# Moving the batch sums, the second step's loads and its normalization in the paired attention steps of a fused attention and gated-MLP kernel

## The chip, the cores and the metric

The kernel runs on one core of a Trainium2 chip. The metric is the device time of one execution in microseconds (us), lower is better. The kernel before takes 518.73 us (median of three runs). Engines are named as the profile names them: PE (TensorE's matmuls), PEld (its weight loads), DVE (VectorE), ACT (ScalarE), POOL (GpSimd), SP (SyncE, which here only issues DMAs).

## The reference

Attention over 4 batches, 8 heads, 768 positions and 64 dimensions, where each query sees the keys within 15 positions and 24 block summaries (the maximum of 32 keys, the mean of 32 values), and behind it a gated network on the 3072 tokens:

```python
k_sum = k.reshape(B, H, nb, block, D).max(axis=3)       # block = 32
v_sum = v.reshape(B, H, nb, block, D).mean(axis=3)
scores_l = scale * np.matmul(q, k.transpose(0, 1, 3, 2))  # masked to |i - j| < 16
scores_s = scale * np.einsum('bhsd,bhnd->bhsn', q, k_sum) + np.log(block)
a = softmax(concatenate([scores_l_masked, scores_s]))
x = a @ concatenate([v, v_sum])                          # 3072 tokens x 512
out = ((x @ w1) * (x @ w2)) @ w3 @ w_out                 # 512 -> 1024 -> 1024 -> 512
```

## The kernel before, in words

Tokens are worked in six units of 512, and a unit has four attention steps, one for each pair of heads: 24 steps in all. A step s stands for `divmod(s, 4)`, unit and pair. One step makes the scores of 512 queries against 120 columns each (96 keys and 24 summaries) on PE (L375), takes the row minima and the mask on DVE (`reduce`, L389), the exponentials and their sums on ACT (`expose`, L403), the reciprocals (`invert`, L408 on ACT and L409 on DVE), multiplies by them (the normalization), transposes the weights on PE (L433), copies the transposes out (`evacuate`, one half on ACT at L438 and one on DVE at L442), and multiplies by the values on PE (`outputs`, L453).

The first eight steps are worked one by one early on. The other sixteen come in pairs: the paired step m, from 4 to 11, holds the steps a = 2m and b = 2m + 1 (`two_steps`). For each m, in program order: `turned(m - 1)` transposes the two steps before and evacuates them, `run` gives PE 18 x 512 columns of the network's matmuls (LEAD), `two_steps` finishes the two steps before with their output products, makes the scores of a and b, and then places the vector work in blocks, with `run(given[0] + LEAD / 2)` (nine matmuls) between them, and at last runs the network until `begins(m + 1) - LEAD`.

The network's matmuls are one long stream (`stream`, taken in order by `run`), on 512 columns each. Up to `CLASSIC` columns it is the folding of the two last weights (w3 and w_out, into `wp`) and the network for the first two units (`gate`, `project`, all at L125); behind it come the other four units in two groups of seven products each (`lanes`, at L736), which read their weights from DRAM tile by tile (`ws`, L781 and L866, six buffers). `begins` sets at which column of the stream a paired step starts: up to m = 8 in equal parts between `TO_SLOTS + LEAD` and `CLASSIC + BEFORE_FAST`, and after that every `BETWEEN` columns. `FAST` is 12,288 columns, or 24 matmuls.

Batches 2 and 3 need their own summaries. Their sixteen loads (four of keys, four of values for each batch, 392 and 512 KB each) and the reductions over them are the later batches' work. `load_batch` issues two loads (L261, L276), `reduce_batch` reduces the two that are under way (L266 for keys, L283 and L284 for values). The loads have two buffers (`raw`), so a load waits until the reduction of the one two before it has read its buffer. Each paired step does both twice: once behind `invert` of step b and once at the middle of the network's stretch. The sixteen are done by m = 7.

How the queues get their order: PE's and POOL's are the program's order. Between `with tc.manual_schedule(engines=vector)` blocks the compiler's scheduler orders ACT, DVE and SP by readiness in its own model and by priority, which is the place in the program; `tc.high_priority(offset=SOONER)` moves an instruction ahead by 400 places. Inside such a block ACT and DVE keep the written order; the instructions of other blocks can stand between them. All loads go through SP's one queue, which issues in order: an issue that waits for its buffer holds up all behind it. Beside the sixteen loads these are a step's values (`fetch_values`, three DMAs at L325, two buffers), queries and keys (`fetch`, L340 and L342, two buffers each), the value summaries (`fetch_means`, L358), and the network's weights. `fill` (L362, POOL) writes the key summaries into a step's keys once these have landed.

The network's background work (`sums_of_gates`, `sums_of_output`, `moving`) makes sums and differences of 512-column tiles on DVE (L121, L634, L685, L691, L938) and casts on ACT, and DVE also adds up what `lanes` leaves in PSUM (L756, L813).

Of the kernel before, what the change touches and what calls it, by code (L numbers as in the profile page):

```python
# [16 lines left out]
ALU = mybir.AluOpType  # L17
# [3 lines left out]
P = 128  # L21
# [31 lines left out]
SOONER = 400  # L53
# [20 lines left out]
def attention_moe(ctx, tc, qG, kW, kT, vP, vW, vB, mask, w1, w2, w3T, wo, out, outT):  # L74
    nc = tc.nc
    B, NPAIR, _, S = kT.shape
# [5 lines left out]
    NI = 2 * NBLK  # L82
# [3 lines left out]
    KR = CUT + NB  # L86
# [40 lines left out]
    def aligned(shape, **more):  # L127


        n = math.prod(shape[1:])  # L130
        step = 32 if more["bufs"] % 4 == 0 else 64
        t = sb.tile([shape[0], -(-n // step) * step], F32, **more)[:, :n]
        return t.rearrange("p (a b) -> p a b", b=shape[2]) if len(shape) == 3 else t
# [185 lines left out]
    def load_values(u, p):  # L319


        v = sb.tile([P, 2, NBLK, P], F32, name="v", bufs=2)

        for g, rows in ((0, slice(0, CUT)), (1, slice(0, CUT - 64)), (1, slice(CUT + NB - 64, KR))):
            nc.sync.dma_start(v[rows, g], vW[u, p, rows, g])  # L325
        return v
# [9 lines left out]
    def load_scores(u, p):  # L336

        q = sb.tile([P, U], F32, name="q")
        k = sb.tile([P, NBLK, COLS], F32, name="k")
        nc.sync.dma_start(q, qG[p, :, u * U : (u + 1) * U])  # L340
        if u:
            nc.sync.dma_start(k, kW[p, :, u * NBLK : (u + 1) * NBLK])  # L342
        return q, k
# [82 lines left out]
    def transposes(sm, **more):  # L426

        tp = [ps.tile([P, 512], F32, name="tp", **more or {"bufs": 2}) for _ in range(2)]
        for j in range(NI):
            for g in range(2):  # L430
                rows = slice(64 * g, 64 * g + 64)
                to, p = tp[g][:KR, j * 64 : j * 64 + 64], sm[rows, j]
                nc.tensor.transpose(to, p, ident[rows, rows])  # L433
        return tp

    def evacuate(tp, second="V"):
        pt = [sb.tile([KR, U], F32, name="pt", bufs=6) for _ in range(2)]
        nc.scalar.copy(pt[0], tp[0][:KR, :U])  # L438
        if second == "A":
            nc.scalar.copy(pt[1], tp[1][:KR, :U])  # L440
        else:
            nc.vector.tensor_copy(pt[1], tp[1][:KR, :U])  # L442
        return pt
# [531 lines left out]
    given, tended = [0.0], [0.0]  # L975

    def tend():


        some = False  # L980
        for works in (tasks, background):
            while works:
                n = next(works[0], 0)
                if n > 0:
                    return True
                if n < 0:
                    break
                works.pop(0)
                some = True
        return some  # L990

    def run(columns):

        while given[0] < columns:
            n = next(stream, 0)
            if n <= 0:
                if n == 0 or not tend():
                    return
                continue
            given[0] += n  # L1000
            if given[0] >= tended[0]:
                tended[0] = max(tended[0] + 4.5 * U, given[0])
                tend()

    def place(s):
        return divmod(s, NPAIR)
# [3 lines left out]
    def fetch(s):  # L1010
        if s < NS:
            inputs[s] = load_scores(*place(s))

    def fetch_values(s):
        if s < NS:
            values[s] = load_values(*place(s))
# [9 lines left out]
    def begin(s):  # L1026
        u, p = place(s)
        sm = sb.tile([P, NI, KR], F32, name="sm", tag="wf", bufs=5)
        mx = aligned([P, 3, NI], name="mx", bufs=4)
        sms[s] = sm, mx  # L1030
        return u, sm, mx, scores(*inputs.pop(s))
# [13 lines left out]
    def load_batch():  # L1045
        for _ in range(2 if later_batches else 0):
            load_, work = later_batches.pop(0)
            under_way.append((work, load_()))

    def reduce_batch():  # L1050
        for work, raw in under_way:
            work(raw)
        under_way.clear()
# [183 lines left out]
    FAST = 3 * U * 4 * KH  # L1237
    LEAD = 18 * U
    PAIRS = range(NFIRST // 2, NS // 2)
    BEFORE_FAST = 0.8 * FAST  # L1240
    BETWEEN = 3.0 * FAST

    def begins(m):

        if m <= NFIRST:
            return TO_SLOTS + LEAD + (CLASSIC + BEFORE_FAST - TO_SLOTS - LEAD) * (m - PAIRS[0]) / (NFIRST - PAIRS[0])
        return CLASSIC + BEFORE_FAST + BETWEEN * (m - NFIRST)

# [9 lines left out]
    def turned(m):  # L1258

        with tc.manual_schedule(engines={engines.Activation, engines.DVE}):  # L1260
            tps = [transposes(sms.pop(p)[0], **SPARE) for p in (2 * m, 2 * m + 1)]
            return [evacuate(tp) for tp in tps]

    def normalize_both(steps):
        for _, sm, mx, _ in steps:
            nc.gpsimd.tensor_tensor(sm, sm, mx[:, 2].unsqueeze(2).broadcast_to([P, NI, KR]), ALU.mult)  # L1266

    def two_steps(m, pts):

        two = (2 * m, 2 * m + 1)  # L1270
        vector = {engines.Activation, engines.DVE}
        with tc.manual_schedule(engines=vector):
            for p, pt in zip(two, pts):
                finish_step(p - 2, pt, **SPARE)
            if m not in PAIRS:
                return
            steps = [begin(p) for p in two]
            (u, sm, mx, sc), (u2, sm2, mx2, sc2) = steps
            reduce(u, 0, sc, sm, mx)
            expose(0, sm, mx)  # L1280
            reduce(u, 1, sc, sm, mx)
        for p in two:
            fetch_values(p)
        for p in two:
            fetch(p + 2)
        for work in EXTRA.get((m, 0), ()):
            work()
        run(given[0] + LEAD / 2)
        with tc.manual_schedule(engines=vector):
            expose(1, sm, mx)  # L1290
            reduce(u2, 0, sc2, sm2, mx2)
            invert(mx)
        run(given[0] + LEAD / 2)
        with tc.manual_schedule(engines=vector):
            expose(0, sm2, mx2)
            reduce(u2, 1, sc2, sm2, mx2)
        normalize_both(steps[:1])
        run(given[0] + LEAD / 2)
        with tc.manual_schedule(engines=vector):
            expose(1, sm2, mx2)  # L1300
            invert(mx2)
            reduce_batch()
        normalize_both(steps[1:])
        load_batch()
        until = begins(m + 1) - LEAD
        run((given[0] + until) / 2)
        for p in two:
            fill(p + 2)
            fetch_means(*place(p), values[p])
        with tc.manual_schedule(engines=vector):  # L1310
            reduce_batch()
        load_batch()
        for work in EXTRA.get((m, 1), ()):
            work()
        run(until)
# [78 lines left out]
```

## Time and profile before

| what | us |
|---|---|
| median of three runs | 518.73 |
| lowest, highest | 518.18, 520.55 |
| the profiled execution, its own time | 516.49 |
| span from its first to its last instruction | 514.7 |
| PE busy | 485.8 (94% of the span) |
| PEld busy | 395.3 (77%) |
| DVE busy | 376.7 (73%) |
| ACT busy | 275.1 (53%) |
| POOL busy | 74.5 (14%) |

The span is counted from the first to the last instruction; 1.79 us of the profiled execution lie around it. A busy PE is not PE at its peak, so its stalls are read from the idle time in front of its instructions and from the granted clock of a stretch, 1.00 being 2.4 GHz and 0.50 being 1.2 GHz. The paired steps lie between about 150 and 350 us of the span.

### The profile page before, as it was taken

To read this page: it belongs to the slowest core of one execution; us is meant where nothing else is said; L and a number is where in the kernel's file an instruction comes from. 1 tells how busy PE (TensorE), PEld (TensorE's weight loads), DVE (VectorE), ACT (ScalarE), POOL (GpSimd) and SP (SyncE) were. 2 spreads that over 40 slices of the span, in tenths; PEclk is the share of its full clock that TensorE was granted. 3 is DMA by queue.
4 is the path that set the end of the run, shared out by engine and by line. 5 is a ranking of instruction groups with operands and counts; after the bars stand their busy time and mean duration, and the time that the engine had idled before them with its cause. 6 is when DMAs were issued, how large, how long until landed. Compare 5 with 4: busy or idle time off the path is not lost. (4 is left out here: it accounts for less than half of the span.)

```text
span 514.7 us, 10411 instructions
## 1 busy us (share of the span) xinstructions
PE 485.8 (94%) x3804; PEld 395.3 (77%) x3804; DVE 376.7 (73%) x889; ACT 275.1 (53%) x738; POOL 74.5 (14%) x101
## 2 busy tenths in 40 slices
PE   0989999999999997899899998999999999999997
PEld 0667777888878886788687886888787888888886
DVE  4969886897616867856988898699999019229972
ACT  5589864875726472727484558451835421522720
POOL 1034523000212313111212304020000000000000
PEclk9999999999999999899899999999999999999999
DMA  8998697999699988869887979998768766556752
GB/s 344 412 408 263 224 356 263 371 401 363 188 300 262 274 260 234 244 205 306 324 276 259 323 263 306 374 293 280 246 217 279 238 200 197 181 193 206 200 190 102
DMA packets 57603, 139.28 MB, mean 271 GB/s; under 512 B 6224, under 2 KB 19280, under 8 KB 54992
## 3 DMA queue, kind: packets, MB, share of 16 engines
q1 hardware_dynamic: 55248, 134.43, 76.9%
q0 software_dynamic: 1152, 2.10, 2.9%
q10 hardware_dynamic: 1152, 2.10, 1.1%
q8 instruction: 30, 0.49, 0.4%
q14 instruction: 21, 0.17, 0.1%
HBM read 105.89 MB, written 32.70 MB: 269 GB/s over the span
## 5 line engine op out<-in xcount | busy, mean ns | idle before, releaser
L736 PE MATMUL ln<-xT,ws 128*128 128x512 f32 x672 | 158.3, 395 | 2.3 <-DMA ws<-wS 2.0
L736 PEld LDWEIGHTS ln<-xT,ws 128*128 128x128 f32 x672 | 126.5, 190 | 30.3 <-ACT hr L754 2.4
L125 PE MATMUL mm<-x,w 128*128 128x512 f32 x384 | 89.3, 392 | 0.2 <-DVE g L527 0.2
L125 PEld LDWEIGHTS mm<-x,w 128*128 128x128 f32 x384 | 71.4, 188 | 16.2 <-DVE g L527 0.6
L403 ACT ACTIVATE sm<-sm,mx 128x120 f32<-128x120 f32 x192 | 73.5, 387 | 9.7 <-DVE mx L389 7.7
L736 PE MATMUL ln<-hT,ws 128*128 128x512 f32 (+1 forms) x348 | 77.2, 383 | 0.1
L736 PEld LDWEIGHTS ln<-hT,ws 128*128 128x128 f32 x348 | 63.7, 188 | 13.5 <-ACT tmp L754 0.5
L756 DVE TENSOR_TENSOR tmp<-ln,tmp 128x512 f32<-128x512 f32 (+1 forms) x53 | 35.7, 675 | 50.5 <-ACT tmp L754 35.1
L125 PE MATMUL mm<-w,w 128*128 128x512 f32 x192 | 50.3, 412 | 14.6 <-ACT w L220 12.0
L638 ACT CAST hT<-hr 128x512 fp32r<-128x512 f32 x56 | 32.1, 621 | 53.4 <-DVE hr L813 42.0
L125 PEld LDWEIGHTS mm<-w,w 128*128 128x128 f32 x192 | 36.2, 195 | 25.7 <-ACT w L220 12.8
L1266 POOL TENSOR_TENSOR sm<-sm,mx 128x960 f32<-128x960 f32 x16 | 29.2, 1827 | 142.0 <-DVE mx L409 133.6
L125 PE MATMUL mm<-wp,h 128*128 128x512 f32 x192 | 45.4, 393 | 0.0
L389 DVE CUSTOM_DVE_ANT_0 sm<-sc,mask_sb 128x120 f32<-128x120 f32 x192 | 40.7, 275 | 6.3 <-PE sc L375 6.3
L125 PEld LDWEIGHTS mm<-wp,h 128*128 128x128 f32 x192 | 35.7, 188 | 8.1 <-ACT o L550 0.4
L121 DVE TENSOR_TENSOR hT<-hr,hT 128x512 fp32r<-128x512 f32 x56 | 35.6, 685 | 3.2 <-ACT hT L638 3.0
L403 ACT ACTIVATION_READ_ACCUMULATOR sm<-sm,mx 128x1 f32 x192 | 36.7, 191 | 0.0
L453 PEld LDWEIGHTS po<-pt,v 120*64 120x64 f32 x768 | 24.4, 141 | 9.4 <-DVE pt L442 4.5
L121 DVE TENSOR_TENSOR w<-wf,w 128x1024 fp32r<-128x1024 f32 (+1 forms) x22 | 25.6, 1165 | 7.8 <-ACT w L220 7.8
L453 PE MATMUL po<-pt,v 120*64 120x64 f32 x768 | 26.8, 227 | 4.4 <-DVE pt L442 4.2
L220 ACT CAST w<-wf 128x1024 fp32r<-128x1024 f32 (+1 forms) x22 | 21.4, 971 | 14.7 <-DVE wf L206 13.4
L176 ACT ACTIVATE wf<-wraw 128x1024 f32<-128x1024 f32 (+1 forms) x22 | 23.2, 1062 | 7.4 <-DMA wraw<-in_wo_dram 3.7
(64 smaller groups left out, 545.2 us busy)
## 6 DMA issues: line engine op xcount, KB each, us to landing
ws<-wS SPq DMA_DIRECT2D x56, 512.0 KB
wraw<-in_w3T_dram SPq DMA_DIRECT2D x8, 1024.0 KB
wraw<-in_w_dram SPq DMA_DIRECT2D x8, 1024.0 KB
wS<-sp SPq DMA_DIRECT2D x16, 512.0 KB
ws<-pS SPq DMA_DIRECT2D x16, 512.0 KB
k<-in_kW_dram SPq DMA_DIRECT2D x20, 368.0 KB
raw<-in_kT_dram SPq DMA_DIRECT2D x16, 392.0 KB
q<-in_qG_dram SPq DMA_DIRECT2D x24, 256.0 KB
```

Source lines behind the costliest of these rows:

```text
L121: eng.tensor_tensor(dst, src, hi.bitcast(F32), ALU.subtract)
L125: nc.tensor.matmul(acc, lhsT=a, rhs=b, start=first and i == 0, stop=last and i == len(terms) - 1)
L176: nc.scalar.activation(f[:, some], words[:, some, 1].bitcast(F32), AF.Prelu, scale=2.0**-112, alpha=-(2.0**32),)
L220: nc.scalar.copy(t[:, 0, some], f[:, some])
L389: nc.vector.tensor_tensor_reduce(out=sm[:, j], in0=sc[h][:, i * KR : (i + 1) * KR], in1=mask_sb[:, 0 if blk == 0 else 2 if blk == BLOCKS - ...
L403: nc.scalar.activation(sm[:, j], sm[:, j], AF.Exp, bias=mx[:, 0, j : j + 1], scale=-1.0, accum_out=mx[:, 1, j : j + 1])
L453: nc.tensor.matmul(po[cols, at : at + 64], lhsT=v[:KR, g, i, cols], rhs=pt[g][:, (h * NBLK + i) * 64 : (h * NBLK + i + 1) * 64], start=Tru ...
L638: nc.scalar.copy(dst[0], src)
L736: nc.tensor.matmul(bank[:, cols], lhsT=x, rhs=y[:, cols], start=c + j == 0 and (split or k in o.first), stop=c == steps - 1 and j == 2 and ...
L756: nc.vector.tensor_tensor(parts[to][:, cols], got, parts[more][:, cols], ALU.add)
L1266: nc.gpsimd.tensor_tensor(sm, sm, mx[:, 2].unsqueeze(2).broadcast_to([P, NI, KR]), ALU.mult)
```

## The change

`BEFORE_FAST` goes from 0.8 to 0.5 of FAST and `BETWEEN` from 3.0 to 3.1, and the middle of the last stretch from 0.5 to 0.6. The evacuation of the transposes gets the higher priority. The first `reduce_batch` of a paired step moves from behind `invert` of step b to behind `reduce` of step b; the first `load_batch` moves with it, one `run` ahead. `fetch_values(b)` moves to behind that `load_batch`, `fetch(b + 2)` to behind the normalization of step b. The normalization of step b goes from POOL to DVE, that of a stays on POOL.

```diff
-    BEFORE_FAST = 0.8 * FAST
-    BETWEEN = 3.0 * FAST
+    BEFORE_FAST = 0.5 * FAST
+    BETWEEN = 3.1 * FAST
+    MIDDLE = 0.6
...
             tps = [transposes(sms.pop(p)[0], **SPARE) for p in (2 * m, 2 * m + 1)]
-            return [evacuate(tp) for tp in tps]
-
-    def normalize_both(steps):
-        for _, sm, mx, _ in steps:
-            nc.gpsimd.tensor_tensor(sm, sm, mx[:, 2].unsqueeze(2).broadcast_to([P, NI, KR]), ALU.mult)
+            with tc.high_priority(offset=SOONER):
+                return [evacuate(tp) for tp in tps]
+
+    def normalize_by(eng, sm, mx):
+        eng.tensor_tensor(sm, sm, mx[:, 2].unsqueeze(2).broadcast_to([P, NI, KR]), ALU.mult)
...
-        for p in two:
-            fetch_values(p)
-        for p in two:
-            fetch(p + 2)
+        fetch_values(a)
+        fetch(a + 2)
...
             reduce(u2, 1, sc2, sm2, mx2)
-        normalize_both(steps[:1])
+            reduce_batch()
+        normalize_by(nc.gpsimd, sm, mx)
+        load_batch()
+        fetch_values(b)
         run(given[0] + LEAD / 2)
         with tc.manual_schedule(engines=vector):
             expose(1, sm2, mx2)
             invert(mx2)
-            reduce_batch()
-        normalize_both(steps[1:])
-        load_batch()
+            normalize_by(nc.vector, sm2, mx2)
+        fetch(b + 2)
         until = begins(m + 1) - LEAD
-        run((given[0] + until) / 2)
+        run(given[0] + MIDDLE * (until - given[0]))
```

## Rows read from the trace of the kernel before

**Rows 1.** The chain that ended last: start, duration (us), what.
```profile
398.07 113.34 PE ln L736 x510
```

**Rows 2.** Waits of PE, 185 to 365 us: total, times, longest (us).
```profile
PE po L453 <- DVE pt L442: 4.2, 2, 4.0
PE tp L433 <- POOL sm L1266: 3.2, 2, 2.5
PE ln L736 <- DMA ws<-wS: 2.0, 1, 2.0
PE sc L375 <- ACT xraw L473: 0.6, 1, 0.6
```

**Rows 3.** Four stretches: length, then busy PE, PEld, DVE, ACT, POOL; clock; DMA.
```profile
207.10:210.50 3.40, 3.33 (x60) 3.22 (x61) 3.37 (x7) 2.39 (x5) 0.00 (x0) 0.51 0.82 251
251.10:255.00 3.90, 3.82 (x23) 3.11 (x24) 3.90 (x8) 1.18 (x2) 1.14 (x5) 0.56 0.66 204
319.80:323.30 3.50, 3.49 (x36) 2.63 (x36) 3.36 (x6) 0.59 (x1) 0.17 (x1) 0.51 1.01 328
337.70:397.80 60.10, 59.98 (x343) 48.59 (x341) 59.87 (x98) 27.25 (x50) 1.79 (x1) 1.00 0.82 265
```

**Rows 4.** Timeline of DVE, from m = 5 into m = 6.
```profile
187.96 0.28 DVE L389 CUSTOM_DVE_ANT_0 sm<-sc,mask_sb 128x120 f32<-128x120 f32 x1
...
192.76 1.17 DVE L283 TENSOR_REDUCE vs<-raw 128x32 f32<-128x1024 f32 x1
...
204.61 1.22 DVE L283 TENSOR_REDUCE vs<-raw 128x32 f32<-128x1024 f32 x1 [2.63 <-DMA raw<-in_vB_dram]
...
206.43 0.69 DVE L442 COPY pt<-tp 120x512 f32<-120x512 f32 x1
```

**Rows 5.** Timeline of SP's issues, m = 5.
```profile
197.10 0.33 SPq L276 DMA_DIRECT2D raw<-in_vB_dram  x1
```

**Rows 6.** Timeline, end of m = 7: reciprocals and normalization of step b.
```profile
245.11 2.50 DVE L938 TENSOR_TENSOR wr<-w 128x512 f32<-128x512 f32 x4
...
246.02 0.21 ACT L408 ACTIVATE mx<-mx 128x8 f32<-128x8 f32 x1
...
248.98 0.19 DVE L409 RECIPROCAL mx<-mx 128x8 f32<-128x8 f32 x1
...
249.34 1.79 POOL L1266 TENSOR_TENSOR sm<-sm,mx 128x960 f32<-128x960 f32 x1 [5.42 <-DVE mx L409]
```

**Rows 7.** Timeline of DVE, end of m = 8 and of m = 11.
```profile
273.27 0.19 DVE L409 RECIPROCAL mx<-mx 128x8 f32<-128x8 f32 x1
...
273.95 2.65 DVE L121 TENSOR_TENSOR xT<-xraw,xT 128x512 fp32r<-128x512 f32 x2
...
338.45 1.93 DVE L685 TENSOR_TENSOR wr<-wr 128x512 f32<-128x512 f32 x1
```

**Rows 8.** Groups by line, whole span: count, busy us, mean ns, idle before.
```profile
L1266 POOL TENSOR_TENSOR sm<-sm,mx 128x960 f32<-128x960 f32 x16 | 29.2, 1827 | 142.0 <-DVE mx L409 133.6 <-PE ln L736 8.4
L634 DVE TENSOR_TENSOR hr<-hr 128x512 f32<-128x512 f32 x32 | 20.9, 684 | 0.1
L422 DVE TENSOR_TENSOR sm<-sm,mx 128x960 f32<-128x960 f32 x4 | 4.8, 1194 | 0.1
```

**Rows 9.** Timeline of SP's issues, m = 10.
```profile
304.38 6.19 SPq L325 DMA_DIRECT2D v<-in_vW_dram  x6
...
314.16 2.62 SPq L781 DMA_DIRECT2D ws<-wS  x4
```

**Rows 10.** Timeline, m = 9: keys for m = 10, and its scores.
```profile
287.66 0.38 SPq L342 DMA_DIRECT2D k<-in_kW_dram  x1
...
293.70 0.27 POOL L362 COPY k<-ks 128x96 f32<-128x96 f32 x1 [0.94 <-DMA k<-in_kW_dram]
...
304.15 1.87 PE L375 MATMUL sc<-k,q 64*64 64x120 f32 x64
```

More of the change, by code (lines that the diff above doesn't have):

```diff
@@ L1261, in turned @@
             tps = [transposes(sms.pop(p)[0], **SPARE) for p in (2 * m, 2 * m + 1)]
-            return [evacuate(tp) for tp in tps]
-    def normalize_both(steps):
-        for _, sm, mx, _ in steps:
-            nc.gpsimd.tensor_tensor(sm, sm, mx[:, 2].unsqueeze(2).broadcast_to([P, NI, KR]), ALU.mult)
+            with tc.high_priority(offset=SOONER):
+                return [evacuate(tp) for tp in tps]
+    def normalize_by(eng, sm, mx):
+        eng.tensor_tensor(sm, sm, mx[:, 2].unsqueeze(2).broadcast_to([P, NI, KR]), ALU.mult)
     def two_steps(m, pts):
-        two = (2 * m, 2 * m + 1)
+        two = a, b = (2 * m, 2 * m + 1)
         vector = {engines.Activation, engines.DVE}
@@ L1276, in two_steps @@
                 return
-            steps = [begin(p) for p in two]
-            (u, sm, mx, sc), (u2, sm2, mx2, sc2) = steps
+            (u, sm, mx, sc), (u2, sm2, mx2, sc2) = [begin(p) for p in two]
             reduce(u, 0, sc, sm, mx)
```

## The prediction, made before the change was run

> **What bounds the kernel now.** I read the chain of work that ended last first. Its last link is one unbroken run of 510 matmuls, 113.34 us long [rows 1]: from 398 us on nothing but PE's own work counts (0.222 us for each matmul of 512 columns), and the change touches nothing there. So a gain must come from PE standing still or running slowly before that. The waits of PE over the paired steps [rows 2] name four places. At the start of m = 6 the output products wait 4.2 us for the transposes' copies by VectorE, and the scores behind them 0.6 us. At the ends of m = 7 and m = 8 the second step's transposes wait 2.5 and 0.6 us (3.2 together, two times) for its normalization by POOL. In m = 10 the network waits 2.0 us for a weight tile. The table by stretches [rows 3] then shows the granted clock behind three of them: 0.51, 0.56 and 0.51 over 3.40, 3.90 and 3.50 us, that is mostly the lower level, 1.2 GHz, after PE had stood still. That costs 3.40 x 0.49 = 1.7, 3.90 x 0.44 = 1.7 and 3.50 x 0.49 = 1.7 us more. Behind the 0.6 us wait no such stretch follows. All that can be won is therefore 4.8 + 1.7 at m = 6, 2.5 + 1.7 at m = 7, 0.6 at m = 8 and 2.0 + 1.7 at m = 10, some 15 us of 516.49. The fourth line of that table is the warning: from 337.7 to 397.8 us VectorE is busy 59.87 of 60.10 us. There it is as full as PE, and what the change adds to it could come back as time.
>
> **The batch sums and the evacuations (m = 6).** VectorE works in order. In m = 5 it finished the minima at 188.2 us, but the first reduction of a batch began only at 192.76, behind `invert` [rows 4]. Each load waits for a buffer that a reduction frees, so the last one was issued at 197.10 [rows 5], and the reduction that needs it stood at the head of VectorE's queue until 204.61, 2.63 of it idle, with the second copy of the transposes behind it at 206.43 [rows 4]. PE waited for that copy. The change removes this twice over. The first two reductions may now follow the minima: up to 192.76 - 188.2 = 4.6 us earlier, and so the two loads behind them, which covers the 2.63 us. And the copies, with 400 places of priority, should stand ahead of the waiting reduction. If the priority alone works, or the earlier loads alone, most of the wait is gone (one reduction of 1.2 us ahead of the copy at most). Lower bound: nothing, if the scheduler puts the copies where they were and the loads stay late. Upper: 6.5. I take 6.4, since two independent causes are removed.
>
> The first reduction now stands in front of the second exponentials, so a late load would hold up the reciprocal and the network's sums behind it. Its load is issued in the step before, with the rest of that stretch, LEAD (18 matmuls, 4.0 us), the output products and the scores (1.87 us [rows 10]) between them, and the load of [rows 5] took 7.5 us to the start of its reduction; I cost this at nothing, and at 2.6 us, as at m = 6, if that room is too small. The middle at 0.6 puts the second reductions and loads later by a tenth of a stretch, about a microsecond, against 4.6 us won.
>
> **The normalization of step b.** It removes eight POOL instructions of 1.83 us and adds eight on VectorE of 1.19 us (the same operation and shape, L422) [rows 8]. For the end of a step it shortens the chain by 0.64 us. At m = 8 the reciprocal starts at 273.27 [rows 7]; 0.19 + 1.19 later the weights are ready, at 274.65, which is within the 0.64 us by which POOL was late. Besides, m = 8 gets 0.1 FAST more, 2.4 matmuls or 0.5 us. I take the whole 0.6. At m = 7 ScalarE was done at 246.23, yet the reciprocal came at 248.98, behind four background sums [rows 6]. With it in the same place, the weights are ready at 250.36 instead of 251.13, 0.8 us sooner; but m = 7 itself becomes shorter, since 0.3 FAST (7.2 matmuls, 1.6 us) is taken out of four steps, 0.4 us each. So the lower bound is 0.4 us. If the reciprocal follows ScalarE at once, the whole 4.2 is gone. The queue's new order isn't to be read from this trace; I take 2.0, about the middle.
>
> What does it cost VectorE? Eight times 1.19 is 9.5 us. But the trace shows that VectorE already pays for POOL's normalization. While POOL ran it at the end of m = 8, two differences took 2.65 us, and at the end of m = 11 one took 1.93 [rows 7], where the usual one takes 0.68 [rows 8]: 1.3 and 1.2 us lost. I find such a loss at five of the eight second normalizations, the two shown in size typical. So in the full stretch behind m = 11 the net cost is 1.19 - 1.25, nothing; over all eight it is some 9.5 - 5.6 = 4 us in places where VectorE has idle time. Range for the full stretch: 0 to 1.2 us.
>
> The Trainium skill, SBUF — State Buffer, section "Who interferes with whom", says that a VectorE instruction with two SBUF inputs shares a read interface with GpSimd and is blocked for the whole of a GpSimd instruction that started first. The two long differences agree with it: both inputs of each lie in SBUF, and 1.2 or 1.3 us is what was left of POOL's 1.83. By that rule the sum stays as it is; with nothing given back it would be 509.9.
>
> **The loads of step b (m = 10).** Of the ten issues of values, queries and keys that stood ahead of the weights in SP's queue, from 304.38 to 314.16 us, 9.8 us long [rows 9], five are b's and now come later in the program: up to 4.9 us off a queue for which PE waited 2.0 us. Upper bound: all of 3.7 us. Lower: nothing, if the scheduler places b's issues ahead of the weights still, for their buffers came free no later than before. I take 2.5, two thirds.
>
> The moved issues count too. The keys of b + 2 must land, and POOL must write the summaries into them, before the next scores. In m = 9, the shortest kind of step, they were issued at 287.66, in use at 293.70 after a wait for the DMA, and the scores came at 304.15 [rows 10]: 10 us of room. Behind the normalization they come perhaps 3 to 5 us later. POOL's queue is shorter by one normalization ahead of that write. No cost, as long as SP isn't held up by 5 us more.
>
> **The spacing.** The paired steps start up to 1.6 us earlier in the stream at m = 8, and as before at m = 11. PE's columns are the same, so by itself that is nothing.
>
> **What comes new.** VectorE's, ScalarE's and SP's orders are made anew by the scheduler over eight steps, and the four stalls cover for others: without them each wait on VectorE or a DMA is met sooner. I allow for two waits of the size that the kernel shows at m = 8 (0.6), and a bit: 1.5 us, between 0 and one more stall with its slow stretch, 3.7 to 4.2.
>
> **Sum.** -6.4 - 2.0 - 0.6 - 2.5 + 0 + 1.5 = -10.0. The profiled execution takes 516.49 us, 1.79 around its span of 514.7; its successor would take 506.5. The median of the runs is 518.73, 2.24 above the profiled execution, and I put the same difference on the forecast: **508.7 us**.
>
> **The rivals.**
> 1. *The keys of the second step come too late* (slower). `fetch(b + 2)` now waits behind `load_batch`, whose issues wait for VectorE's reductions, and behind b's values. From issue to use the keys took 6.0 us, so the case decides if b's are issued later than 304.15 - 6.3 = 297.8 on the clock of [rows 10], 10 us behind their place before, where I expect 3 to 5. Then PE stands in front of the scores; two microseconds of standing cost 3.7 with the slow stretch, as at m = 10. Four steps of it cost 14.8: 518.7 - 10.0 + 14.8 = 523.5. For it: SP's issues in m = 10 took 9.8 us for ten [rows 9]. Against it: the room of 10 us. Chance 0.15.
> 2. *The change doesn't do what it says.* The scheduler leaves the copies behind the batch reductions, or another reduction stands in front of them in another step, and the spared waits turn up a step further on. Then only m = 8 and parts of m = 7 are won, and 1.5 lost: about 518. For it: queues ordered from a model of readiness put a reduction first whose load came 2.63 us late [rows 4]. Against it: two causes are removed. Chance 0.14.
> 3. *Only the copies and m = 8 are mended*; m = 7 and m = 10 stay, since their causes are the order of the reciprocal and of the weights' issues: -7.0 + 1.5, or 513. Chance 0.25.
> 4. *VectorE becomes the bound* in the full stretch: 1.2 us at m = 11, and as much at each of m = 8 to 10 if nothing is given back: -10.0 + 4.8, or 513.5. Against it: the two long differences [rows 7]. Chance 0.06.
> 5. The forecast, 505 to 512, has 0.34; all four stalls gone and none new, 503.7, has 0.06.
>
> **The numbers.** Half a per cent, 2.6 us, is about what a measurement of this kernel can tell from no change. Faster are cases 3, 4 and 5: 0.71. The same is most of case 2: 0.13. Slower is case 1 with a little of 2: 0.16. The range for 8 in 10 goes from 504.5, just above the case of no new wait, to 519.5, where the case of no change ends; the forecast's own is 505 to 512.
>
> **What the profile would show.** In the waits of PE: no wait for the transposes' copies, and the one for the normalization, now by VectorE, under a microsecond. The granted clock stays at 1.00 where rows 3 has 0.51. The first batch reductions start within a microsecond of the last minimum. Differences of 2 us disappear where POOL no longer runs. In m = 10 the weights are issued before 312 us of the old clock. The prediction is wrong if a new wait of over 2 us stands in front of scores or transposes, if VectorE's copies still come 4 us or more behind the transposes, or if PE waits for VectorE's sums around 398 us by much more than now.

## The result, and the profile after

The changed kernel takes 514.23 us (median of 4 runs, 513.55 to 514.91) against 518.75 before: a ratio of 0.9907, 95% interval 0.9878 to 0.9936. Measured again, beside the experiments, it gave 0.9891 (0.9855 to 0.9926). (A ratio leaves disturbed runs out, and so isn't quite the quotient of two medians.) It is faster by about one per cent. The direction holds and the time lies in the wide range (504.5 to 519.5), not in the forecast's own (505 to 512): of the 10 us of its sum less than half came. The profiled execution takes 514.64 us with a span of 512.9, only 1.9 us less than the one before.

The waits of PE in the changed kernel, 170 to 365 us (total, times, longest), which answer to [rows 2]:

```profile
PE sc L375 <- issue: 3.2, 2, 2.2
PE sc L375 <- ACT xraw L473: 1.8, 2, 1.1
PE po L453 <- issue: 1.4, 1, 1.4
PE ln L736 <- ACT tmp L754: 0.6, 1, 0.6
PE ln L736 <- ACT hr L754: 0.5, 1, 0.5
PE tp L433 <- DVE sm L1267: 0.5, 1, 0.5
```

The three largest waits of before are gone under their names: none for the transposes' copies, 0.5 us for the normalization, none for a weight tile. In their place stand four waits in front of scores. They begin at 181.0 (2.24 us long) and 183.7 (1.09) in m = 5, where before there was none, and at 208.7 (0.94) and 210.1 (0.70) in m = 6. The first is over 2 us long and stands in front of scores, one of the signs by which the prediction called itself wrong. The stretches behind them, against [rows 3] (length; busy PE, PEld, DVE, ACT, POOL; clock; DMA):

```profile
184.00:188.00 4.00, 3.27 (x34) 2.73 (x35) 3.92 (x25) 2.83 (x9) 0.00 (x0) 0.57 0.80 250
210.00:216.00 6.00, 5.30 (x43) 4.24 (x43) 4.67 (x35) 5.01 (x23) 0.00 (x0) 0.72 0.94 266
246.00:250.00 4.00, 3.54 (x42) 2.72 (x42) 4.00 (x7) 1.17 (x2) 0.39 (x2) 1.00 0.98 379
```

Behind both groups of new waits the granted clock falls to the lower level for a part of the stretch (means of 0.57 and 0.72), and that costs about 4.00 x 0.43 = 1.7 and 6.00 x 0.28 = 1.7 us. At m = 7 it stays at 1.00.

**Why PE waits at m = 5.** The timeline of ScalarE in the changed kernel, m = 5 and, behind the dots, m = 6 (start, us, what, idle before and its releaser):

```profile
176.91 0.62 ACT L675 CAST sp<-wr 128x512 fp32r<-128x512 f32 x1 [2.60 <-DVE wr L685]
181.54 0.62 ACT L675 CAST sp<-wr 128x512 fp32r<-128x512 f32 x1 [4.00 <-DMA wS<-sp]
182.58 0.58 ACT L473 COPY xraw<-po 128x512 f32<-128x512 f32 x1
184.10 0.58 ACT L473 COPY xraw<-po 128x512 f32<-128x512 f32 x1
...
206.81 0.62 ACT L675 CAST sp<-wr 128x512 fp32r<-128x512 f32 x1 [4.75 <-DMA wS<-sp]
208.98 0.59 ACT L473 COPY xraw<-po 128x512 f32<-128x512 f32 x1
```

The scores of step b need the PSUM bank that the output products left, and ScalarE's copy of these (L473, in `keep_raw`) frees it. ScalarE works in order, and the second cast of the background (L675, in `stationary`) stands ahead of the copy. It writes a tile `sp` whose buffer a store (L681) must first have read. The copy could only start at 182.58, and PE went on at 183.26. The store's place in SP's queue, in the changed kernel:

```profile
170.02 1.84 SPq L276 DMA_DIRECT2D raw<-in_vB_dram  x2
171.91 0.49 SPq L681 DMA_DIRECT2D wS<-sp  x1
```

and in the kernel before, with the cast and the copy on ScalarE:

```profile
168.47 0.34 SPq L681 DMA_DIRECT2D wS<-sp  x1
170.58 2.39 SPq L276 DMA_DIRECT2D raw<-in_vB_dram  x2
...
178.06 0.62 ACT L675 CAST sp<-wr 128x512 fp32r<-128x512 f32 x1 [0.58 <-DVE wr L687]
...
180.12 0.59 ACT L473 COPY xraw<-po 128x512 f32<-128x512 f32 x1 [0.35 <-PE po L453]
```

The store went from in front of the two loads of a batch to behind them, 3.44 us later (171.91 against 168.47). Before, the second cast had no wait for the store: what it waited for last, 0.58 us, was a sum of VectorE (L687). In the changed kernel it waits 4.00 us for the store and starts at 181.54 instead of 178.06.

The runs below agree. In the six others that have both the sums' move and the second cast ahead of the first copy (l0, p2, s2, l2, l3, t1), this store is issued behind the two loads too, at 170.7 to 172.9, the second cast waits 3.5 to 5.0 us for it, and m = 5 has waits of 2.5 to 4.1 us. In p1, p3, p4, l1 and s3, which leave the sums at their old place, it is issued ahead of the loads, at 167.8 to 169.5, the second cast waits at most 0.6 us, and m = 5 has 0 to 1.8 us. Those smaller waits come with a first cast that waits for a late sum of VectorE (4.9 us in l1, 4.6 in p3, 5.4 in s3).

The moved sums themselves came as forecast. VectorE's first reduction of m = 5 starts at 189.21 instead of 192.76, right behind the last minimum. At m = 7 a later one shows the price of the new place:

```profile
189.21 1.22 DVE L283 TENSOR_REDUCE vs<-raw 128x32 f32<-128x1024 f32 x1
...
245.39 1.22 DVE L283 TENSOR_REDUCE vs<-raw 128x32 f32<-128x1024 f32 x1 [0.89 <-DMA raw<-in_vB_dram]
246.53 0.19 DVE L409 RECIPROCAL mx<-mx 128x8 f32<-128x8 f32 x1
```

It waits for its load, and the reciprocal of the step stands behind it. The groups by line (count, busy us, mean ns) show that VectorE paid little for the eight normalizations:

```profile
L121 DVE TENSOR_TENSOR sp<-wr,sp 128x512 fp32r<-128x512 f32 x24 | 16.1, 685 | 6.3 <-ACT sp L675 6.3
L1267 DVE TENSOR_TENSOR sm<-sm,mx 128x960 f32<-128x960 f32 x8 | 9.3, 1168 | 0.2
```

VectorE is busy 377.4 us instead of 376.7, with 9.3 us of new work in it; the mean of the first group was 836 ns before.

### The profile page after: what moved, and what is told of

It is laid out like the page before. It is cut to its first block, busy times and chain, and to the rows that moved or that the text cites. A ratio compares the mean times of both kernels' runs of the same rounds, so it can differ in the third digit from the quotient of the medians.

```text
span 512.9 us, 10388 instructions
## 1 busy us (share of the span) xinstructions
PE 485.9 (95%) x3804; PEld 394.7 (77%) x3804; DVE 377.4 (74%) x897; ACT 274.1 (53%) x738; POOL 60.8 (12%) x93
## 4 chain that ended last, share of the span: by engine, by line
PE 63%; DVE 16%; DMA 10%; ACT 7%; issue 2%; SPq 1%; POOL 0%; ACTq 0%; DVEq 0%; POOLq 0%
PE ln L736 34%; PE mm L125 21%; PE po L453 3%; DMA wS<-sp 3%; PE sc L375 3%; DVE hT L121 3%; ACT sm L403 2%; PE tp L433 2%; DVE tmp L756 2%; DVE wf L206 2%; DVE w L121 2%; DMA wr<-pR 2%; DVE xT L121 1%; DMA wraw<-in_w_dram 1%; ACT w L220 1%
## 5 line engine op out<-in xcount | busy, mean ns | idle before, releaser
L736 PE MATMUL ln<-xT,ws 128*128 128x512 f32 x672 | 156.4, 392 | 0.9 <-ACT hr L754 0.5
L736 PEld LDWEIGHTS ln<-xT,ws 128*128 128x128 f32 x672 | 125.2, 188 | 28.8 <-ACT hr L754 0.9
L125 PE MATMUL mm<-x,w 128*128 128x512 f32 x384 | 91.5, 398 | 0.1
L125 PEld LDWEIGHTS mm<-x,w 128*128 128x128 f32 x384 | 73.1, 192 | 16.7 <-issue 0.6
L375 PE MATMUL sc<-k,q 64*64 64x120 f32 x768 | 26.3, 273 | 5.2 <-issue 3.2
L675 ACT CAST sp<-wr 128x512 fp32r<-128x512 f32 x24 | 14.7, 621 | 28.7 <-DMA wS<-sp 8.8
L1267 POOL TENSOR_TENSOR sm<-sm,mx 128x960 f32<-128x960 f32 x8 | 14.7, 1832 | 119.1 <-DVE mx L409 80.3
```

The lines of the kernel that those rows point to most:

```text
L125: nc.tensor.matmul(acc, lhsT=a, rhs=b, start=first and i == 0, stop=last and i == len(terms) - 1)
L375: nc.tensor.matmul(sc[h][64 * g : 64 * g + 64, i * KR : (i + 1) * KR], lhsT=q[rows, i * P + 64 * g : i * P + 64 * g + 64], rhs=k[rows, i, ...
L675: nc.scalar.copy(to[:, 0], raw)
L736: nc.tensor.matmul(bank[:, cols], lhsT=x, rhs=y[:, cols], start=c + j == 0 and (split or k in o.first), stop=c == steps - 1 and j == 2 and ...
L1267: eng.tensor_tensor(sm, sm, mx[:, 2].unsqueeze(2).broadcast_to([P, NI, KR]), ALU.mult)
```

## The experiments

All runs, with PE's waits in their profiled executions at the starts of m = 5 and 6, at the transposes that end m = 7 and m = 8, and in m = 10, network and transposes (us). Waits under 0.2 us are left out, and each entry is that of one execution. Ratios are to the kernel before, measured beside each; its medians there were 517.06 to 518.75, and its single runs went from 513.5 to 522.4.

| kernel | median | ratio (95%) | m = 5 | m = 6 | m = 7 | m = 8 | m = 10 |
|---|---|---|---|---|---|---|---|
| before | 518.73 | 1 | 0 | 4.8 | 2.5 | 0.6 | 2.0 |
| changed | 514.23 | 0.9907 (0.9878–0.9936) | 3.3 | 1.6 | 0.5 | 0 | 0.5 |
| l0, changed again | 512.93 | 0.9891 (0.9855–0.9926) | 3.0 | 0.7 | 2.5 | 0 | 0 |
| p1, priority alone | 516.5 | 0.9979 (0.9944–1.0013) | 0 | 5.6 | 2.0 | 0.6 | 2.5 |
| p2, moves alone | 520.27 | 1.0042 (1.0004–1.0081) | 3.4 | 3.1 | 0.6 | 1.9 | 0 |
| p3, normalization alone | 517.31 | 1.0009 (0.9971–1.0047) | 1.4 | 4.1 | 1.0 | 0.7 | 1.8 |
| p4, spacing alone | 518.96 | 1.0042 (1.0007–1.0077) | 0.7 | 6.6 | 0 | 0.7 | 0 |
| l1, without the moves | 519.0 | 1.001 (0.9981–1.0039) | 1.3 | 6.5 | 0 | 0 | 0 |
| l2, without the spacing | 517.82 | 0.999 (0.9966–1.0014) | 4.1 | 1.4 | 0.8 | 2.0 | 0 |
| l3, without the normalization | 520.19 | 1.006 (1.0025–1.0096) | 3.3 | 2.7 | 1.5 | 0 | 1.3 |
| s2, of the moves only the sums | 513.83 | 0.9924 (0.9886–0.9961) | 2.5 | 1.6 | 0 | 0 | 3.2 |
| s3, of the moves only the loads | 516.51 | 0.9988 (0.9954–1.0022) | 1.8 | 5.3 | 0 | 0 | 0 |
| q, stores with priority | 521.56 | 1.0051 (1.0022–1.008) | 6.0 | 0 | 3.0 | 0 | 0 |
| t1, hold at m = 5, 6 in the lead | 529.66 | 1.021 (1.0157–1.0263) | 4.0 | 0 | 0 | 0 | 0 |
| t4, hold in lead and stretch | 527.73 | 1.0185 (1.0133–1.0236) | 0 | 2.6 | 0 | 0 | 0 |
| u5, hold at m = 5, caught up | 513.48 | 0.9904 (0.9867–0.994) | 0 | 4.4 | 0 | 0 | 0.7 |
| u6, hold at m = 5, 6, caught up | 508.93 | 0.9865 (0.9814–0.9915) | 0 | 0.6 | 3.1 | 0 | 0 |
| v2, u6 again | 508.79 | 0.9858 (0.9821–0.9896) | 0 | 1.4 | 1.4 | 0 | 0 |
| v1, the hold of u6 on before | 515.47 | 0.9969 (0.9946–0.9992) | 0.2 | 0.7 | 3.2 | 0.6 | 2.4 |

**Each part alone.** On the kernel before, p1 makes only the first of these edits and p4 only the last two; p3 puts only the normalization of step b on VectorE, ahead of `reduce_batch`.

```diff
-            return [evacuate(tp) for tp in tps]
+            with tc.high_priority(offset=SOONER):
+                return [evacuate(tp) for tp in tps]
...
-        normalize_both(steps[1:])
+            nc.vector.tensor_tensor(sm2, sm2, mx2[:, 2].unsqueeze(2).broadcast_to([P, NI, KR]), ALU.mult)
...
-    BEFORE_FAST = 0.8 * FAST
-    BETWEEN = 3.0 * FAST
+    BEFORE_FAST = 0.5 * FAST
+    BETWEEN = 3.1 * FAST
...
-        run((given[0] + until) / 2)
+        run(given[0] + 0.6 * (until - given[0]))
```

p2 makes only the moves; both normalizations stay on GpSimd:

```diff
-        for p in two:
-            fetch_values(p)
-        for p in two:
-            fetch(p + 2)
+        fetch_values(two[0])
+        fetch(two[0] + 2)
...
             reduce(u2, 1, sc2, sm2, mx2)
+            reduce_batch()
         normalize_both(steps[:1])
+        load_batch()
+        fetch_values(two[1])
...
             invert(mx2)
-            reduce_batch()
         normalize_both(steps[1:])
-        load_batch()
+        fetch(two[1] + 2)
```

p1: 

> The kernel before with the evacuation's priority alone. VectorE's order then differs at one place: both copies of m = 6 stand ahead of the reduction that waited for its load. Theory A (the new waits come from the moved sums and loads, through stores that are issued late in SP's queue): the 4.2 + 0.6 us wait at m = 6 and its slow stretch go, nothing new comes, some 6 us less than before, about 512.5. Rival B (a stall taken away only meets the next wait on VectorE or a DMA): the reduction's idle time moves in front of the network's sums, PE waits elsewhere, less than 2 us gained.

p2: 

> The kernel before with the moves alone: first reductions and loads one block earlier, step b's values, queries and keys later. Normalization, spacing and priority as before. Theory A: the wait at m = 6 for the copies goes, but the scores of m = 5 wait some 3 us and those of m = 6 some 1.5 us for ScalarE, which stands behind a cast that waits for a store of SP's queue; 3 us less than before, 515 to 517. Rival C (the spacing and the later middle bring those waits): no waits in front of the scores of m = 5 here, 511 to 513.

p3: 

> The kernel before with the normalization of step b on VectorE alone. Theory A: the waits of the transposes at m = 7 and m = 8 shrink to under 1 us together and the slow stretch behind m = 7 goes, some 4 us less than before, 514 to 516; VectorE's busy time hardly grows, since the differences blocked by POOL get short. Rival D (VectorE becomes the bound): the waits of PE around 398 us grow by 1 us or more, and the gain is under 2 us.

p4: 

> The kernel before with 0.5, 3.1 and the middle at 0.6 alone. Theory A: nothing by itself, 517 to 520, since the waits at m = 6 and m = 7 stay. Rival C: new waits in front of the scores of m = 5, slower by 3 us; or, with the order of the weights' loads in m = 10 changed, that wait goes and it is 3 us faster.

No part alone makes the kernel faster. p1 shows why the wait at m = 6 doesn't go with the first cause that is named for it. The timeline of DVE, ACT and PE in p1:

```profile
206.38 1.22 DVE L283 TENSOR_REDUCE vs<-raw 128x32 f32<-128x1024 f32 x1 [2.03 <-DMA raw<-in_vB_dram]
...
208.92 1.34 ACT L675 CAST sp<-wr 128x512 fp32r<-128x512 f32 x2 [3.44 <-DVE wr L685]
210.17 0.58 ACT L473 COPY xraw<-po 128x512 f32<-128x512 f32 x1
...
210.85 0.63 PE L375 MATMUL sc<-k,q 64*64 64x120 f32 x2 [4.69 <-issue]
```

VectorE's copies of the transposes are on time now (their wait fell to 0.43 us). But the background's sum (L685) still stands behind the late reduction, ScalarE's cast waits for the sum, the copy of the products stands behind the cast, and the scores miss their bank: 4.69 us. Two chains led from one late reduction to PE, and the second became visible when the first was cut. PE waits 5.6 us at m = 6 in p1, 4.8 before.

**One part left out.** l0 is the changed kernel, unedited. l1 undoes the moves in it (the diff of p2 backwards), l2 the spacing (0.8, 3.0 and 0.5 again), and l3 the normalization:

```diff
-            normalize_by(nc.vector, sm2, mx2)
+        normalize_by(nc.gpsimd, sm2, mx2)
         fetch(b + 2)
```

l0: 

> The changed kernel itself once more, beside the kernel before and the three variants of it below, on one chip. 0.6 to 1.2% less than before if the first measurement holds, and PE's waits in front of the scores of m = 5 and m = 6 again (theory A). If those waits were a chance of one execution (rival E), this profile shows none over 0.5 us.

l1: 

> The changed kernel without the moves: sums, loads, values, queries and keys at the old places; VectorE's normalization, the spacing and the priority stay. Theory A (the moves take the reduction's wait out of m = 6, but bring the late stores): the waits in front of the scores of m = 5 go, the 2.6 us wait of the reduction in m = 6 is back and with it 4 to 5 us of PE waiting for ScalarE's copies; within 0.3% of the changed kernel. Rival F (the moves carry the gain): no faster than before.

l2: 

> The changed kernel with 0.8, 3.0 and the middle at 0.5. Theory A: the spacing does nothing by itself; within 0.3% of the changed kernel. Rival G (the spacing makes the room in which the moves and VectorE's normalization pay): half of the gain or more is gone, waits at the ends of m = 7 and m = 8 or for the weights in m = 10 come back.

l3: 

> The changed kernel, but with the normalization of step b on GpSimd again; moves, spacing and priority stay. Theory (the gain belongs to moves and spacing together, the normalization only shortens a step's end by 0.64 us): 1 to 3 us slower than the changed kernel, with PE waiting 1 to 3 us for GpSimd at the end of one or two of m = 7 and 8, and differences of over 1.9 us back on VectorE. Rival A (the normalization carries its full 2.6 us and more by what comes behind): 4 us slower or more, the gain gone. Rival B (VectorE's 9.5 us do cost something): same or faster than the changed kernel.

Each of the three takes the whole gain away: moves, spacing and normalization are needed together. The table shows where their stalls lie: without the moves m = 6 has 6.5 us, without the spacing m = 8 has 2.0 and m = 5 4.1. Why none of the three can be spared is not shown beyond that. For l3 Rival A came true. Among its waits of PE are two for GpSimd, at m = 7 and in m = 10, 2.6 us together, where the changed kernel waits 0.5 us for VectorE:

```profile
PE tp L433 <- POOL sm L1267: 2.6, 2, 1.5
```

And in the full stretch VectorE's differences run beside GpSimd again (timeline of DVE in l3):

```profile
340.29 2.03 DVE L687 TENSOR_TENSOR wr<-wr 128x512 f32<-128x512 f32 x1
```

A difference that takes 0.68 us elsewhere takes 2.03 here, beside a GpSimd instruction from 339.99 to 341.78; at 342.57 PE waits 1.0 us for a sum, which the changed kernel doesn't. The Trainium skill, SBUF — State Buffer, section "Who interferes with whom", has a VectorE instruction with two inputs in SBUF blocked while a GpSimd instruction that reads SBUF and began first is under way; the trace agrees, with 1.35 us lost.

l0 differs from the first profile of the same kernel at m = 7, 2.5 us against 0.5, and VectorE's timeline says why:

```profile
245.99 1.22 DVE L283 TENSOR_REDUCE vs<-raw 128x32 f32<-128x1024 f32 x1 [3.04 <-DMA raw<-in_vB_dram]
247.13 0.20 DVE L409 RECIPROCAL mx<-mx 128x8 f32<-128x8 f32 x1
```

The reduction that now stands ahead of the reciprocal waited 3.04 us for its load here, 0.89 there.

**Which of the moves.** In the changed kernel, s2 puts the loads of step b back at their old place:

```diff
-        fetch_values(a)
-        fetch(a + 2)
+        for p in two:
+            fetch_values(p)
+        for p in two:
+            fetch(p + 2)
...
         load_batch()
-        fetch_values(b)
...
-        fetch(b + 2)
```

s3 does the opposite: `reduce_batch` stands behind the normalization of step b and `load_batch` behind that, and the loads of step b keep their new place.

s2: 

> The changed kernel with only half of its moves: the first batch sums and their loads stay at their new place, the loads of step b (values, queries and keys) are back at the old one. Theory (the sums' move mends m = 6 and the loads' move mends m = 10): m = 6 without a wait of over 2 us, but a wait for a weight tile of 1 to 2.5 us in m = 10 with its slow stretch; 2 to 4 us slower than the changed kernel, some 515 to 517. Rival (the loads of step b must be out of the way for the batch loads to be early at all): m = 6's or m = 5's wait of over 3 us is back as well, 518 or more. Second rival (spacing alone mends m = 10): same time as the changed kernel.

s3: 

> The changed kernel with the other half of its moves: values, queries and keys of step b at their new place, the first batch sums and their loads back behind the reciprocal of step b. Theory (the sums' move carries the gain, as the run with it alone was as fast as the changed kernel): m = 6 has a wait of 4 to 5 us in front of products or scores again, no wait for a weight tile in m = 10; 516 to 519, the gain gone. Rival (either move is enough): within 2 us of the changed kernel.

The sums' move carries the gain: s2 can't be told from the changed kernel, and s3 has none. In s3 two reductions in front of the background's sums wait 1.66 and 1.48 us for their loads, and m = 6 has 5.3 us. What the loads' move does in m = 10 is less clear. The timeline of s2 there, SP, DVE and PE:

```profile
306.07 0.42 SPq L949 DMA_DIRECT2D wr<-pR  x1
...
312.55 0.69 DVE L685 TENSOR_TENSOR wr<-wr 128x512 f32<-128x512 f32 x1 [2.09 <-DMA wr<-pR]
...
315.61 1.62 PE L736 MATMUL ln<-xT,ws 128*128 128x512 f32 x3 [3.23 <-ACT hr L754]
```

The ten issues stand in one row again, from 297.32 us on, with a load of the background behind them. VectorE waits for that load, ScalarE's copy comes late, and PE waits 3.2 us, where the changed kernel has 0.5. The place of the issues isn't shown to be the reason. In the changed kernel the same load is issued only 0.76 us sooner (305.31), and VectorE waits longer for it:

```profile
313.13 0.69 DVE L685 TENSOR_TENSOR wr<-wr 128x512 f32<-128x512 f32 x1 [5.47 <-DMA wr<-pR]
```

There PE gets to this place some 2.8 us later than in s2 (315.2 against 312.4), which is about what the two waits differ by. Nor does any kernel that has the spacing without the loads' move (p4, l1, s2) wait 0.2 us or more for a weight tile in m = 10.

**The store first.** q puts the issue of the store (L681) under the high priority:

```diff
+            with tc.high_priority(offset=SOONER):
-            nc.sync.dma_start(to_dram(k), to.bitcast(F32))
+                nc.sync.dma_start(to_dram(k), to.bitcast(F32))
```

> The changed kernel with the stores of the background sums ahead of the batch loads in SP's queue (priority on that issue alone). Theory A: the store that ScalarE's cast waits for in m = 5 is issued 8 to 10 us sooner, the cast no longer waits 4 us, the waits of 2.2 + 1.1 us in front of the scores of m = 5 go and those of m = 6 shrink; 3 to 5 us less than the changed kernel. Rival H (ScalarE's queue is late for another reason, or the batch loads now come late): no difference, the waits in front of the scores stay or turn up at the copies of m = 6.

The theory fell in this form. No cast waits for the store that stood behind the loads any more, and the wait in front of the first copy is down to 0.4 us, but the second stands behind another cast, whose store was under way (ScalarE's timeline in q):

```profile
183.57 0.58 ACT L473 COPY xraw<-po 128x512 f32<-128x512 f32 x1
...
189.01 0.62 ACT L675 CAST sp<-wr 128x512 fp32r<-128x512 f32 x1 [4.21 <-DMA wS<-sp]
189.54 0.58 ACT L473 COPY xraw<-po 128x512 f32<-128x512 f32 x1
```

PE waits 6.0 us at m = 5. So the wait depends on which cast stands ahead of the copies, not on the place of one store alone.

**The cast out of the way.** t1 and t4 hand out no background steps around m = 5 and 6, t1 in the 18 x 512 columns in front of the products, t4 in the last part of the stretch before as well:

```diff
-            if given[0] >= tended[0]:
+            if given[0] >= tended[0] and not quiet[0]:
...
+            quiet[0] = m in (5, 6)
             run(given[0] + LEAD)
+            quiet[0] = False
...
+        quiet[0] = m + 1 in (5, 6)
         run(until)
+        quiet[0] = False
```

t4: 

> The changed kernel, with the background sums held back around the starts of m = 5 and m = 6: none of their steps is handed out in the 18 x 512 columns in front of the output products, nor in the last part of the stretch before. ScalarE's queue then has both copies of the output products of m = 5 ahead of any cast of the background. Theory (the new wait of m = 5 is ScalarE standing at a cast whose buffer a late store frees, with the copies behind it): the waits in front of the scores of m = 5, 1.9 to 2.2 and 1.1 us, are gone with the slow clock behind them (about 1.5 us), so 3 to 4.5 us below the changed kernel, near 510. Rival (something else is late at the same place, the products or the scores' own inputs): the wait stays at 2 to 3 us under another name, no change in time. Second rival: the sums that are held back come late for the weights, or stand in front of the copies of m = 6 or m = 7; then 0 to 3 us slower.

t1: 

> The changed kernel, with the background sums held back only in the 18 x 512 columns in front of the output products of m = 5 and m = 6. ScalarE's queue around m = 5 stays as it is, with a cast ahead of the first copy and one between the two; at m = 6 no cast stands ahead of the copies any more. Theory: m = 5 keeps its 2 to 3 us, m = 6's 0.9 and 0.7 us go; 0.5 to 2 us below the changed kernel. Rival (m = 6's waits have another cause): no change at m = 6, same time.

The waits of PE in t4:

```profile
PE ln L736 <- ACT tmp L754: 8.8, 2, 5.3
PE ln L736 <- DMA ws<-pS: 4.6, 1, 4.6
PE sc L375 <- issue: 1.9, 1, 1.9
```

and the largest of t1:

```profile
PE ln L736 <- DMA ws<-pS: 14.8, 1, 14.8
```

In t4 both copies stand ahead of the casts, and m = 5 has no wait at all, although the store is issued behind the two loads as before (170.93): it is the cast ahead of the copy through which the late store reaches PE. The cause of the wait is shown. t1, whose queue of ScalarE keeps the cast ahead there, keeps 4.0 us. But the background ends later, its weights are wanted from 355 us on, and both kernels are some 2% slower than before.

**Held and caught up.** u6 and u5 hold as t4 does (u5 for m = 5 alone), count the steps kept back, and hand out two at a time behind the hold until the count is zero:

```diff
+                if owed[0] > 0:
+                    owed[0] -= 1
+                    tend()
+            elif given[0] >= tended[0]:
+                tended[0] = max(tended[0] + 4.5 * U, given[0])
+                owed[0] += 1
```

u6: 

> The changed kernel, with the background held back around the starts of m = 5 and m = 6 and two of its steps handed out at a time behind that until the held ones are made up for. In ScalarE's queue the copies of both stand ahead of the background's casts. Theory (the waits at m = 5 and 6 are what the forecast lacked): both waits gone, no late weights behind 340 us, 507 to 510 us, some 3 to 6 us below the changed kernel. Rival (the stall is only passed on: background steps in a hurry take VectorE's or ScalarE's place elsewhere): the waits at m = 5 and 6 are gone, but others of the same sum stand at m = 7 to 11, and the time is that of the changed kernel or above, 513 to 518.

u5: 

> The same with the hold around m = 5 alone. At m = 6 two casts of the background stand ahead of the copies. Theory: m = 5's wait (2 to 3 us and the slow clock) is gone, m = 6's grows to 2 to 4 us, since a cast waits there for a store that was issued late: 0 to 2 us below the changed kernel. Rival: m = 6's wait doesn't grow, and 3 us or more are won.

u6 takes 508.93 us, by its ratio 1.35% below before, and its median is 0.9% below that of u5 on the same chip. The waits of PE in u6, the largest two:

```profile
PE tp L433 <- DVE vs L284: 3.1, 1, 3.1
PE sc L375 <- ACT xraw L473: 0.6, 1, 0.6
```

Its stretches around m = 5 and in m = 7:

```profile
178.00:190.00 12.00, 12.00 (x158) 10.30 (x154) 11.52 (x47) 11.09 (x43) 2.00 (x2) 1.00 0.86 264
239.00:248.00 9.00, 5.89 (x46) 4.70 (x46) 8.78 (x15) 1.76 (x3) 0.95 (x2) 0.81 0.98 345
```

And ScalarE's start of m = 5:

```profile
178.75 0.59 ACT L473 COPY xraw<-po 128x512 f32<-128x512 f32 x1 [1.73 <-PE po L453]
...
180.37 0.62 ACT L675 CAST sp<-wr 128x512 fp32r<-128x512 f32 x1
```

PE is busy for all of 178 to 190 us at the full clock. What remains is m = 7, where a reduction ahead of the reciprocal waits for its load. u5 passes the stall on: m = 5 has none, m = 6 4.4 us, and the time is that of the changed kernel.

**The hold without the change.** v1 makes the edits of u6 on the kernel before; v2 is u6 again.

v1: 

> The kernel before with only the hold of the background around the starts of m = 5 and 6, made up for right behind it; none of the change's edits. Theory (the wait that the hold takes away comes with the change): in before no cast waits for a store ahead of the copies of m = 5, and at m = 6 the copies of the transposes still stand behind the batch reduction; the waits of 4 us there, of 2.5 us at m = 7 and of 2 us in m = 10 stay, 515 to 520, within 0.5% of before. Rival (the hold clears VectorE and ScalarE at m = 6 by itself, whatever the change): m = 6's wait is gone, 511 to 514.

v2: 

> The changed kernel with the hold around m = 5 and 6, made up for right behind it, once more. If the first measurement holds: 507 to 511, ratio 0.982 to 0.99, no wait of over 1 us in front of the scores of m = 5 and 6. If it was the spread between runs: 512 to 515, as the changed kernel.

v2 repeats u6. v1's time is near before's, as expected, but not for the reason given: its wait at m = 6 is down to 0.7 us, as the rival had it, while m = 7, 8 and 10 keep 3.2, 0.6 and 2.4. The hold alone gives 0.3%, and 0.9969 x 0.9907 = 0.9876 lies within the intervals of u6 and v2. So the two add up, and what u6 has more than the changed kernel is not shown to be the change's own gain set free.

## Why the prediction was right in direction and wrong in size

By its own steps, from the profiled executions (us against before; waits, and the slow clock behind them from the stretches above):

| step | forecast | changed | u6 |
|---|---|---|---|
| m = 5 and 6 | -6.4 | 3.3 + 1.6 + 3.4 - 6.5 = +1.8 | 0.6 - 6.5 = -5.9 |
| m = 7 | -2.0 | 0.5 - 4.2 = -3.7 | 3.1 + 1.7 - 4.2 = +0.6 |
| m = 8 | -0.6 | -0.6 | -0.6 |
| m = 10 | -2.5 | 0.5 - 3.7 = -3.2 | -3.7 |
| new waits elsewhere | +1.5 | 1.4 + 0.6 = +2.0 | 0.5 + 0.6 - 0.3 = +0.8 |
| sum | -10.0 | -3.7 | -8.8 |
| profiled execution | | 514.64 - 516.49 = -1.9 | 507.89 - 516.49 = -8.6 |

(The 0.3 in u6's column is a wait for VectorE's sum near 398 us that the kernel before has too.) The column of u6 is no proof of the change's own terms: v1, the hold without the change, comes to 0.2 + 0.7 - 6.5 = -5.6 at m = 5 and 6.

**The step that failed is "The batch sums and the evacuations (m = 6)", the -6.4.** Its reading of the named wait was right: the copies of the transposes no longer wait, and the reductions start 3.55 us earlier. What failed is "The change removes this twice over" and "If the priority alone works, or the earlier loads alone, most of the wait is gone". The two causes weren't two ways out of one chain, since a second chain led to PE: reduction, background sum, ScalarE's cast, copy of the products, bank of the scores (p1). And the move that mended the late reductions put the loads of a batch ahead of a store, whose lateness came back through that cast, at m = 6 and one step earlier: 4.9 us of waits and 3.4 of slow clock at m = 5 and 6, where 6.5 were to go. The step counted what the moved issues wait for and what waits for them, but not whose issue they now stand in front of in SP's queue. What the priority does within the whole change is not shown: every variant of the changed kernel keeps it.

**The normalization of step b.** -2.0 for m = 7 was a middle between ends, and the runs lie at both: 0.5 us of wait in one profile, 2.5 in l0, 3.1 in u6 and 1.4 in v2. The reason is one that the prediction priced at nothing or 2.6 us under m = 6, a late load in front of the reciprocal. m = 8 went as said. That VectorE pays almost nothing net is borne out by 0.7 us more of busy time; l3 shows that the part is worth more than its two terms of 2.6 us, since without it the whole gain is gone.

**The loads of step b.** -2.5, measured -3.2 at its place, but not shown to be this part's: l1 has no wait there without it, nor has p4, which makes the new spacing alone. By the medians it can't be told from nothing (s2). So far the nearness of the number is luck.

**The spacing.** It was put at nothing "by itself", and by itself it gives nothing (p4, 1.0042). But the sum has no term for its share in the others, and without it the gain is gone (l2, 0.999).

**New waits.** +1.5, measured 2.0, apart from those at m = 5 and 6.

**The rivals.** The keys of step b never came late: those of m = 9 were issued at 281.20 and 286.77. On the clock of the changed kernel, where the next scores start at 300.51, the point that decides is 300.51 - 6.3 = 294.2, some 7 us later (rival 1). The time is nearest to that of rival 3 (513), whose mechanism (copies mended, m = 7 and 10 left) isn't what happened. Rival 2 comes nearest: "the spared waits turn up a step further on"; here they turn up at the same step and the one before. VectorE did not become the bound (rival 4).

The 1.8 us between the rows' sum and the profiled execution of the changed kernel belong to that one execution. In l0, the same kernel, the rows give 3.0 + 0.7 + 1.7 - 6.5 = -1.1 at m = 5 and 6, 2.5 + 1.7 - 4.2 = 0 at m = 7, -0.6 at m = 8, -3.7 in m = 10 and +0.1 elsewhere. With 1.3 us more of idle time of PE before 150 us that is -4.0, and the profiled execution shows 512.38 - 516.49 = -4.1. In the first one the 1.8 lie in PE's busy time (485.9 us against 485.8, with one slow stretch fewer), and no view names the reason.

What stays open: why moves, spacing and normalization are each needed; why p4's runs are 0.4% slower than before, while its profiled execution (515.94) is not; and why a store takes up to 10 us to land (171.91 to at most 181.54). More buffers for `sp` were not tested.

## What to carry to other kernels

Before you book a wait as gone, follow every chain from its cause to the engine that waits: cut the first, and look up what the next instruction in line would then wait for. When an issue moves in an in-order queue, list what it now stands in front of, stores too, and follow these to the buffers that they free. Where parts of a change each seem worth microseconds, measure it with each left out: here three parts gave nothing alone and one per cent together, and without any of them all of it was gone.

## What the runs showed that was not expected

- Withholding the background's steps in two leads of 18 x 512 columns (t1) cost one wait of 14.8 us some 170 us later. Withholding more of them but handing the same steps out two at a time right behind (u6) left no such wait.
- The store behind two 512 KB loads held its buffer for 9.6 us (issued at 171.91, the cast at 181.54); another, behind two loads of keys, for 6.0 (200.81 and 206.81).
- Single runs of the kernel before spread over 1.7% (513.5 to 522.4 us), and the same load was 0.89 or 3.04 us late in two executions of the changed kernel.
